# All 24 units make their first feed-forward layer in columns, with a new hand order of the work

## The chip, the cores and the metric

The kernel runs on one core of one Trainium2 chip. A core has five engines that run side by side, each working through its own instructions in order: PE (TensorE: matrix products), DVE (VectorE), ACT (ScalarE), POOL (GpSimd) and SP (SyncE, which here only issues transfers). 16 DMA engines move data between the chip's memory and the core. Products land in PSUM, eight banks that POOL cannot reach; all else lives in SBUF. The metric is the time of one execution on the device, in microseconds (us).

## What is computed

A linear attention with a decaying state (4 batches, 8 heads, 768 steps, head dimension 48), and behind it a feed-forward block with a softmax-weighted activation and a layer norm:

```
for t in range(S):                          # attention, for each batch and head
    y[t]  = r[t] @ (state + outer(u * k[t], v[t]))
    state = w[t][:, None] * state + outer(k[t], v[t])
x    = y of all heads side by side          # 3072 x 384
h    = x @ w_in                             # 3072 x 1024: the first layer
solu = h * softmax(h)
ln   = (solu - mean(solu)) / sqrt(var(solu) + 1e-6) * g_ln
out  = ln @ w_out                           # 3072 x 384
```

## The kernel before

The work is cut into 24 units of 128 tokens: unit i is chunk i // 4 of batch i % 4, and a unit needs the state that the unit four before it left. A unit goes through some forty steps. No loop orders them: the string `ORDER` is a list of words, written in the order in which the instructions are made, and `InOrder` (line 71) holds each engine to that order. So each engine does its words in the order of the string and waits where a word's data or buffer is not ready yet. A word is a step's name and the unit; behind the point stand the PSUM bank (for PE) or the engine that does it (a ACT, d DVE, p POOL; for loads, a means that ACT's queue issues it, else SP's). The words that matter here:

- `LW LK LR LV`: loads of w, k, r, v of a unit, 0.197 MB each, into rings of seven buffers. `LI0` to `LI2` load the three pieces of w_in (0.52 MB each), `LO` the halves of w_out (0.79 MB each); `wi` turns a piece of w_in into bf16, `gw` multiplies a piece of w_out by the gain, `mn`, `mc` and `ce` subtract its column mean.
- `lw` (logarithm of the decay, ACT), `cum` (its running sum, two products on PE), `ex` (exponential, ACT), `kp` (k and r scaled by it, DVE), `krk`, `krr` (both turned, PE) and `kr` (copied out of PSUM). For eight units `kt` turns them by a DMA of SP's queue instead.
- `M` (scores, 8 products), `m` (copied and masked; where ACT copies, POOL masks in a word `sel`), `vb` (v in bf16), `p q qh dg dv` (the bonus u, on POOL and DVE), `Y` (the attention's output, 12 products; a letter i means that the bonus is added by one product more on PE, n that `y` adds it on DVE), `y` (copied out), `S et st` (the state).
- `X` (y turned by PE into the bank) and `xT` (copied out); `xt` turns y by a DMA of SP instead, for units 21 to 23.
- `H`: the first layer. In columns it is 24 products, 8 blocks of 128 features by 3 pieces, and a unit's features lie on the partitions. `e` is its exponential (ACT), `he` h times e (DVE), `hq` the squares of he (ACT), `ea` the sum of the halves of e (POOL). `HA`/`HB` with `EA`, `DA`, `QA` and their like do the same for unit 23 in two halves.
- `Oa`, `Ob`: the two halves of the second layer. For a unit in columns each feature block gives a product on he (385 columns), one of width 1 on hq, and one on ea for every second block: the sums of e and of the squares come out of the same accumulation.
- `sq qm lv rs`: mean, variance and inverse root, on ACT and DVE; `o` scales the output, `out` stores it (SP).

Units 17 to 21 (set `by_rows`, those with a word `ht`) make the first layer in token rows: 6 products of 512 columns, tokens on the partitions. Then the sums of e and of the squares come out of ACT's own accumulation (`be_t`, `s2_t`; a word `sv` squares the sum of e), no `ea` is needed, and a DMA of SP's queue (`ht`, `turned_he`) turns he into columns for `Oa` and `Ob`, which then consist of the products on he alone.

PE's order in the last part before reads:

```
X18.4 Y20.n6 Y19.n0 M21.1 M22.3 H18.6 X20.0 Oa16.2 X19.1 Ob16 Y21.n1 H19.4 M23.6 Y22.n3 H20.0 Oa17.6
Y23.n7 Ob17 Oa18.3 H21.4 Ob18 H22.0 Oa19.2 HA23.6 Ob19 Oa20.7 HB23.3 Ob20 Oa22.4 Oa21.0 Ob22 Oa23.7 Ob21 Ob23
```

Of the kernel before, what the change touches and what calls it, by code (L numbers as in the profile page):

```python
# [8 lines left out]
F32 = mybir.dt.float32  # L9
# [12 lines left out]
ih0 LW0.a LU0.a LW2 LW5 LR2.a LW1.a LK1.a lw2 LW3 hot10.0 cum2.0 LR0.a LK2 LK0 p2 lw0 lw5 lw1 ik0 us0.3 cum0.4 ex2  # L22
LK3.a kp2 hot7.2 krk2.0 p0 LR3 krr2 LR1.a ex0 kp0 LV0.a kr2.d cum1.6 krk0.5 uc0 krr0 q0 p3 q2 ex1 lw3 hot2.0 cum3.3
LV2.a kr0.d LV3.a kp1 p1 M0.0 ex3 LK6 m0.a hot2.2 krk1.2 LW6 M2.6 LG0.a krr1 LR5 q1 qh1 LR6 dg0 LW7 kp3 krk3.1 dg2
krr3 LO1 vb0.p kr1.d LR7 cum5.4 vb2.p LK5.a LV1.a lw6 M1.2 m2.d vb3.p dv2 kr3.a hot3.0 cum6.6 ex6 dg1 m1.d hot1.0
M3.0 LW4.a S0.2 m3.d gs0.3 q3 S3.0 ex5 kp5 sel0 dv0 LK4.a p5 kp6 hot2.1 krk5.1 gc0 et3 lw7 Y2.n3 LK7 cum7.4 LO0
krk6.6 krr5 st3 y2.d et0 vb1.a st0 LR4.a gw5.a ex7 kr5.d dv1 LI1 Y0.i0 hot1.3 Y1.n2 LW9 y0.a lw4 q5 krr6 p6 LI2.a
hot2.1 cum4.0 ex4 kr6.d dg3 M5.6 q6 S1.3 LW8 kp7 gw6.a krk7.4 y1.d et1 X1.2 dv3 qh6 LI0.a Y3.i5 gw4.a kp4 p4 gw1.a
m5.d y3.a krr7 gw7.a hot1.0 X0.7 gw2.a kr7.d krk4.6 M6.0 X3.4 q4 krr4 xT0.d LV5.a gw0.d xT1.a LR9 gw3.d st1 xT3.a
LK11 mn0.5 kr4.d M4.3 p7 LR8 dg6 wi2.p LW11 S2.2 LV4.a wi0.d qh5 m6.a LK8 X2.1 LV6 mc0 xT2.a wi1.p ce4.d H3.6 dg4  # L30
m4.d ce5.p ce7.p LR11 vb5.a lw9 ce3.p e3 dg5 LK9 H0.0 H1.4 he3 vb4.a e0 ce2.p dv5 lw8 he0 e1 hq0.a Y5.n7 S4.6 y5.d
ce0.p et4 S5.3 ce6.p he1 H2.0 dv4 LV8 et5 Y4.n7 lw11 cum8.4 ce1.p st4 y4.d Oa0.6 ea1.p vb6.p p8 et2 hq1.a X5.7 st5
Ob0 st2 e2 ea2.p LW10 ex8 xT5.d LW12 he2 Oa1.7 cum11.2 sq0 qm0 kp8 cum9.0 Ob1 hq3.a lv0 rs0 ex11 ex9 sq1 o0.d lw10
S6.4 kp11 qm1 H5.5 q7 LR10 lv1 qh7 out0 et6 kp9 rs1 cum10.2 LK10 vb8.p o1.a M7.0 st6 ea3.p Oa3.7 e5 X4.4 dg7 ex10
LR12 m7.d Ob3 xT4.d hq2.a q8 dv6 sq3 p11 out1 lw12 H4.0 he5 qm3 qh8 lv3 rs3 Oa2.5 kp10 LK12 cum12.3 e4 o3.d krk11.6
dg8 sel6 krk8.2 krk9.7 hq5.a ex12 p10 LV7 krr8 q11 krr9 he4 kr8.d kp12 krr11 Ob2 kr9.a vb7.p M8.1 S8.0 LW14 S7.3
krk10.7 p9 sq2 qm2 lw14 ea4.p LV11 out3 q9 LR14 krk12.4 m8.d lv2 rs2 et8 krr10 o2.a st8 dv7 hq4.a kr10.d LW17 krr12
qh11 kr11.a Y6.n5 y6.d kr12.d cum14.0 Oa4.7 et7 st7 Y7.n2 ex14 y7.d lw17 LK14 ea5.p q10 out2 Ob4 vb11.a sq4 LW13
LV9 kp14 LR17 LK17 dv8 M9.5 m9.a M11.3 LV10 LK13 qm4 Y8.n2 S11.1 lv4 m11.d et11 Oa5.0 rs4 qh9 o4.a p12 lw13 cum17.4
ex17 dg10 y8.d p14 X7.7 krk14.3 X6.6 vb10.p out4 xT6.a dv10 Ob5 vb9.a krr14 dg11 st11 sq5 LR13 xT7.d kp17 kr14.a  # L40
M10.1 qm5 m10.d lv5 sel9 rs5 LW15 cum13.6 o5.d H6.4 ex13 M12.2 dg9 e6 H7.0 LV12 kp13 dv11 m12.a X8.6 Y11.n7 q12 e7
qh12 S9.2 he6 dv9 out5 LW16 LK15 y11.d S10.5 et9 xT8.a vb12.a lw15 M14.3 Y9.i6 Y10.n7 et10 lw16 he7 st9 st10
cum15.0 m14.d q14 sel12 ea7.p y9.a S12.2 hq7.a dg12 et12 H8.5 y10.d LR15 LV13 ex15 e8 p13 Oa7.3 dv12 X9.7 LR16 kp15
Ob7 he8 hq6.a krk15.4 LW18 ea8.p q13 sq7 qm7 st12 Y12.n0 xT9.a LW21 p15 y12.d krr15 LK16 lv7 LV14 lw18 cum16.5 p16
ea6.p rs7 o7.d X10.7 xT10.d H9.1 hq8.a kr15.d Oa8.7 X11.0 dg14 cum18.3 Ob8 ex16 e9 xT11.a lw21 kp16 he9 LR18 sq8
Oa6.5 X12.6 q15 vb14.p M15.1 ex18 out7 LV15 LK18 qm8 dg13 lv8 vb15.p vb13.p Ob6 m15.d rs8 o8.a sq6 qm6 S15.7
krk16.0 xT12.a lv6 LK21 kp18 rs6 et15 o6.a LR21 cum21.1 out8 S13.6 p18 q16 st15 et13 krr16 ex21 H11.3 hq9.a LW19
e11 LV17 ea9.p p17 st13 out6 kr16.d H12.5 kt13 LV16 kp21 lw19 dv14 ea11.p H10.0 dg15 LW20 he11 e12 he12 q17 q18
hq11.a dg16 dv15 LK19 Y14.n7 e10 LR19 ea12.p Oa9.2 y14.d hq12.a Oa11.3 M16.4 he10 M13.6 vb16.p Ob9 m16.a lw20 dv13
m13.d cum19.0 qh18 sq9 sel16 ex19 Ob11 sq11 LK20 LR20 qm9 kt17 lv9 qm11 rs9 lv11 kp19 ea10.p o9.a rs11 Y13.n7  # L50
vb17.p o11.a out9 S14.4 Y15.n6 et14 S16.5 et16 y15.d y13.d cum20.0 Oa12.2 out11 ex20 X15.3 st16 dg17 dv16 kp20 Ob12
X13.7 hq10.a p21 dv17 LW22 xT15.d sq12 p19 S17.5 qm12 xT13.a Y16.n0 M17.6 q19 st14 lv12 H13.3 rs12 o12.a y16.d
X16.2 LV18 lw22 m17.d et17 cum22.6 dg18 H15.0 e13 ex22 LK22 e15 vb18.p out12 LR22 xT16.d he13 kp22 he15 hq13.a
Oa10.2 H16.3 p20 LW23 lw23 q20 e16 X14.6 Ob10 st17 sq10 ea13.p ea15.p LK23 kt19 qh20 xT14.d qm10 hq15.a q21 LR23
he16 Y17.n0 Oa13.7 cum23.5 y17.d lv10 kt18 rs10 ex23 o10.d Ob13 sq13 qm13 lv13 rs13 X17.4 H14.0 o13.a kt20 e14
xT17.d kp23 M19.3 m19.d he14 M18.5 dv18 p23 m18.a Oa15.7 S18.2 Ob15 et18 dg21 p22 out10 sq15 M20.5 ea14.p qm15
hq14.a m20.d H17.0 dg20 out13 lv15 sel18 Y18.n4 LV20 LV19 st18 rs15 dg19 vb19.p kt21 vb20.p o15.a e17 Oa14.5 y18.d
dv20 dv19 S19.3 Ob14 X18.4 et19 he17 q22 hq16.a kt22 qh22 ea16.p Y20.n6 Y19.n0 st19 sq14 qm14 y20.d M21.1 xT18.a
q23 out15 M22.3 lv14 LV21 H18.6 y19.d m21.d kt23 vb21.p rs14 dg22 sv17 X20.0 Oa16.2 qh23 X19.1 Ob16 dv21 o14.a
out14 m22.d e18 he18 dg23 xT19.a LV22 xT20.a hq17.a sq16 sv18 Y21.n1 qm16 lv16 H19.4 vb22.p M23.6 y21.d dv22 Y22.n3  # L60
H20.0 rs16 m23.d LV23 y22.d ht17 o16.a e19 Oa17.6 hq18.a vb23.p ht18 xt21 dv23 Y23.n7 Ob17 e20 Oa18.3 he19 y23.d
out16 sq17 qm17 lv17 sv19 xt22 H21.4 hq19.a ht19 xt23 he20 rs17 Ob18 e21 ht20 H22.0 o17.d out17 sq18 qm18 Oa19.2
HA23.6 he21 lv18 rs18 e22 hq20.a Ob19 o18.d he22 EA23 sq19 Oa20.7 HB23.3 Ob20 sv20 qm19 hq22.a ht21 lv19 DA23 sq20
qm20 rs19 lv20 out18 o19.d ea22.p rs20 EB23 hq21.a Oa22.4 Oa21.0 o20.d QA23.d out19 DB23 Ob22 sq22 qm22 sv21 lv22
out20 Oa23.7 QB23.d Ob21 rs22 o22.a sq21 qm21 out22 lv21 rs21 Ob23 sq23 qm23 lv23 rs23 o21.d out21 o23.a out23
# [36 lines left out]
def kernel(  # L102
# [130 lines left out]
    diagonal = consts.tile([C, C], BF16)  # L233
# [335 lines left out]
    words = ORDER.split()  # L569
    squared = {int(word[2:].split(".")[0]) for word in words if word[:2] in ("hq", "QA")}  # L570

    def output(i, part):
        L = live[i]
        e, he, hq, o_ps = e_t[i % NWK], he_t[i % NWK], hq_t[i % NWK], L["o_ps"]
        for f in range(part * KF // 2, (part + 1) * KF // 2):
            if i in by_rows:
                pe.matmul(o_ps[:, :DM + 1], lhsT=he[:, f, :], rhs=w2[:, f, :], start=(f == 0), stop=(f == KF - 1))
                continue
            last = f == KF - 1 and i not in squared
            pe.matmul(o_ps[:, :DM + 1], lhsT=he[:, f, :], rhs=w2[:, f, :], start=(f == 0), stop=last and i in added,  # L580
                      skip_group_check=True)
            if i not in added:
                pe.matmul(o_ps[:, DM + 1:DM + 2], lhsT=e[:, f, :], rhs=inv_col, start=False, stop=last,
                          skip_group_check=True)
            elif f % 2 == 0:
                pe.matmul(o_ps[:, DM + 1:DM + 2], lhsT=ea_t[i % NWK][:, f // 2, :], rhs=inv_col, start=False, stop=False,
                          skip_group_check=True)
            if i in squared:
                pe.matmul(o_ps[:, DM + 2:], lhsT=hq[:, f, :], rhs=one_col[:, :1], start=False, stop=(f == KF - 1),
                          skip_group_check=True)  # L590
            else:
                pe.matmul(L["g_ps"], lhsT=he[:, f, :], rhs=he[:, f, :], start=(f == 0), stop=(f == KF - 1))

    def output_a(i, x):
        if i in squared:
            live[i]["o_ps"] = bank([C, DM + 3], F32, x, "o_ps")
        else:
            both = bank([C, 2, 512], F32, x, "o_ps")
            live[i]["o_ps"], live[i]["g_ps"] = both[:, 0, :DM + 2], both[:, 1, :C]
        output(i, 0)  # L600
# [11 lines left out]
    def variance(i, x):  # L612
        if i not in squared:
            dve.scalar_tensor_tensor(out=diagonal, in0=live[i]["g_ps"], scalar=sq_t[i % NWK][:, 0:1], in1=ident,
                                     op0=SUB, op1=MULT, accum_out=qm_t[i % NWK])
            return
# [34 lines left out]
    for word in words:  # L651
# [33 lines left out]
```

## Time and profile before

| | us |
|---|---|
| median of 3 runs (153.36 to 154.04) | 153.54 |
| the profiled execution | 153.27 |
| its span, from the first instruction to the last | 151.5 |
| busy: PE, DVE, ACT, POOL | 133.4, 122.1, 119.9, 115.2 |
| DMA: read, written | 22.03 MB, 4.72 MB |
| first product of a first layer (H3) starts | 38.24 |
| last output (Ob23) ends on PE | 147.2 |

The profile numbers times from the start of the span. A row of an engine's instructions in order of time has the start, the duration, the engine, the line, what is written and read, and in brackets the idle time of the engine ahead of it with what ended that. All instructions carry the line of `InOrder`'s call (L87), so they are told apart by what they write and read: `ps<-xT,win_sb` is H in columns, `ps<-win_sb,xT` H in rows, `ps<-w,he` the wide product of the second layer, `ps<-one_col,hq` that on the squares, `e<-ps` the exponential, `hq<-win_f` or `hq<-he` the squares of a unit in rows or in columns. Products overlap, so what one costs is the time from its start to the start of the next.

### The profile page before, as it was taken

To read this page: it belongs to the slowest core of one execution; us is meant where nothing else is said; L and a number is where in the kernel's file an instruction comes from. 1 tells how busy PE (TensorE), PEld (TensorE's weight loads), DVE (VectorE), ACT (ScalarE), POOL (GpSimd) and SP (SyncE) were. 2 spreads that over 40 slices of the span, in tenths; PEclk is the share of its full clock that TensorE was granted. 3 is DMA by queue.
4 is the path that set the end of the run, shared out by engine and by line. 5 is a ranking of instruction groups with operands and counts; after the bars stand their busy time and mean duration, and the time that the engine had idled before them with its cause. 6 is when DMAs were issued, how large, how long until landed. Compare 5 with 4: busy or idle time off the path is not lost.

```text
span 151.5 us, 4749 instructions
## 1 busy us (share of the span) xinstructions
PE 133.4 (88%) x1853; PEld 95.2 (63%) x1858; DVE 122.1 (81%) x215; ACT 119.9 (79%) x258; POOL 115.2 (76%) x154
## 2 busy tenths in 40 slices
PE   6977877549999999996999999979999999996980
PEld 2333444425996788775888689658867675565650
DVE  5047998397899999997999999879688998868550
ACT  3355656734899999996999989988988877997782
POOL 7159997686999999995999999999986599603000
PEclk9999999955999999999999999999999999999997
DMA  5999999999993489998989999999988997957533
GB/s 100 258 259 259 259 326 299 376 315 220 197 208 58 100 183 240 209 205 197 222 165 211 212 225 135 229 200 219 234 164 210 174 204 159 202 149 151 123 146 114
DMA packets 119800, 30.75 MB, mean 203 GB/s; under 512 B 115289, under 2 KB 119394, under 8 KB 119778
## 3 DMA queue, kind: packets, MB, share of 16 engines
q1 hardware_dynamic: 101792, 26.06, 80.8%
q10 hardware_dynamic: 17986, 4.40, 12.6%
q8 instruction: 14, 0.23, 0.6%
q14 instruction: 8, 0.07, 0.1%
HBM read 22.03 MB, written 4.72 MB: 176 GB/s over the span
## 4 chain that ended last, share of the span: by engine, by line
PE 25%; POOL 21%; DMA 20%; ACT 13%; ACTq 6%; issue 5%; DVE 4%; SPq 3%; DVEq 0%; POOLq 0%
PE ps L87 25%; DMA kr_in<-in_r_dram 7%; ACTq L87 6%; POOL ea L87 5%; DMA v_in<-in_v_dram 5%; POOL q L87 4%; SPq L87 3%; POOL w L87 3%; DMA kr_in<-in_k_dram 3%; ACT e L87 3%; POOL dv L87 3%; DMA xT<-y 3%; POOL p L87 2%; DMA w_in<-in_w_dram 2%; DVE kp L87 2%
## 5 line engine op out<-in xcount | busy, mean ns | idle before, releaser
L87 PE MATMUL ps<-w,he 128*128 128x385 bf16 x192 | 42.9, 325 | 0.0
L87 DVE TENSOR_TENSOR kp<-ps,kr_in 128x768 bf16<-128x768 f32 x24 | 22.8, 953 | 14.2 <-ACT ps L87 5.7
L87 PE MATMUL ps<-xT,win_sb 128*128 128x128 bf16 x456 | 28.1, 219 | 2.4 <-DVE kp L87 1.3
L87 POOL TENSOR_TENSOR p<-kr_in 128x384 bf16<-128x384 f32 x24 | 24.0, 1004 | 7.3 <-DMA kr_in<-in_k_dram 4.2
L87 PEld LDWEIGHTS <-win_sb 128*128 128x128 bf16 x456 | 26.1, 98 | 3.9 <-DMA xT<-y 1.5
L87 ACT ACTIVATE e<-ps 128x1024 bf16<-128x1024 f32 (+1 forms) x25 | 24.6, 985 | 2.5 <-PE ps L87 0.9
L87 POOL TENSOR_TENSOR ea<-e 128x512 bf16<-128x512 bf16 x17 | 19.6, 1157 | 7.4 <-ACT e L87 7.4
L87 PE MATMUL ps<-one_col,hq 128*128 128x1 bf16 x152 | 24.9, 164 | 0.0
L87 DVE TENSOR_TENSOR he<-ps,e 128x1024 bf16<-128x1024 f32 (+1 forms) x20 | 23.3, 1165 | 1.2 <-ACT e L87 0.9
L87 DVE TENSOR_TENSOR m<-ps,keep 128x1024 bf16<-128x1024 f32 x18 | 21.8, 1216 | 0.8 <-PE ps L87 0.8
L87 POOL TENSOR_TENSOR q<-p,u_bc 128x384 bf16<-128x384 bf16 x24 | 21.9, 915 | 0.6 <-DMA kr_in<-in_k_dram 0.2
L87 ACT ACTIVATE ps<-ps 128x768 f32<-128x768 f32 x24 | 19.0, 800 | 4.0 <-PE ps L87 2.4
L87 PEld LDWEIGHTS <-he 128*128 128x128 bf16 x192 | 18.2, 96 | 5.8 <-DVE st L87 0.2
L87 POOL TENSOR_TENSOR dv<-vb,dg 128x384 bf16<-128x384 bf16 x24 | 19.9, 832 | 1.3 <-ACT vb L87 1.0
L87 ACT ACTIVATE hq<-he 128x1024 bf16<-128x1024 bf16 x18 | 18.9, 1051 | 0.0
L87 ACT ACTIVATE lw<-w_in 128x384 bf16<-128x384 f32 x24 | 12.3, 522 | 6.8 <-issue 5.3
L87 PEld LDWEIGHTS <-kp 128*128 128x128 bf16 x208 | 13.0, 99 | 7.3 <-DVE kp L87 5.8
L87 PEld LDWEIGHTS <-hq 128*128 128x128 bf16 x152 | 11.6, 96 | 5.5
L87 PE MATMUL ps<-ident,kp 128*128 128x128 bf16 x128 | 11.0, 225 | 3.4 <-DVE kp L87 3.4
L87 PEld LDWEIGHTS <-kr 64*128 64x128 bf16 (+1 forms) x272 | 10.2, 96 | 5.4 <-issue 1.9
L87 POOL CAST vb<-v_in 128x384 bf16<-128x384 f32 x18 | 8.9, 506 | 4.5 <-DMA v_in<-in_v_dram 4.0
L87 PE MATMUL ps<-warm 128*128 128x512 bf16 x28 | 9.8, 468 | 2.0 <-DVE kp L87 1.7
(94 smaller groups left out, 286.3 us busy)
## 6 DMA issues: line engine op xcount, KB each, us to landing
out_dram<-o SPq DMA_DIRECT2D x24, 192.0 KB, 2.9
w_in<-in_w_dram SPq DMA_DIRECT2D x21, 192.0 KB, 4.4
kr_in<-in_k_dram SPq DMA_DIRECT2D x20, 192.0 KB, 4.1
kr_in<-in_r_dram SPq DMA_DIRECT2D x20, 192.0 KB, 4.4
v_in<-in_v_dram SPq DMA_DIRECT2D x18, 192.0 KB, 4.2
wout_f<-in_moe_w_out_dram SPq DMA_DIRECT2D x2, 768.0 KB, 7.1
v_in<-in_v_dram ACTq DMA_DIRECT2D x6, 192.0 KB, 5.5
win_f<-in_moe_w_in_dram ACTq DMA_DIRECT2D x2, 512.0 KB, 6.4
```

What stands on the lines that cost most here:

```text
L87: made = make(*args, **kwargs)
```

## The change

No word `ht`, `sv` is left, so `by_rows` is empty: units 17 to 21 go in columns like all others, and each gets a word `ea`. Unit 0, which summed e by eight products of its own, gets an `ea` too (`ea` is then there for all but unit 23). Unit 20's y is turned by DMA (`xt20` for `X20`, `xT20`). The whole string `ORDER` is another permutation: 941 words instead of 950. In it

- DVE, ACT and POOL exchange words: of the 24 `vb`, ACT has 12 (6 before) and POOL 12; `kr` 2 on ACT and 14 on DVE (4 and 12); `gw` 7 on ACT and 1 on POOL (6 on ACT, 2 on DVE); `ce` 4 and 4 on DVE and POOL (1 and 7); `wi` on ACT, POOL, POOL (POOL, POOL, DVE); `xT` 14 on ACT and 6 on DVE (12 and 9); `qh` 10 (12). The six `sel` are for other units.
- `Y1` and `Y10` add the bonus on PE and `Y9` no longer does.
- The weights' loads stand elsewhere among the others: `LO1 LV2 LO0` and `LI0 LI1 LW8 LI2` follow each other, where before it was `LO1`, five loads, `LO0`, and `LI1 LW9 LI2 LW8 LI0`. `LR5` goes to ACT's queue, `LW4` to SP's.
- `hot`, products that nobody reads, which keep PE busy at the start: 33 instead of 31.

In the code only dead paths go: the product of he with itself, which would give the squares of units without `hq` (none), and its buffer `diagonal`.

```diff
-    words = ORDER.split()
-    squared = {int(word[2:].split(".")[0]) for word in words if word[:2] in ("hq", "QA")}
...
-            last = f == KF - 1 and i not in squared
-            pe.matmul(o_ps[:, :DM + 1], lhsT=he[:, f, :], rhs=w2[:, f, :], start=(f == 0), stop=last and i in added,
+            pe.matmul(o_ps[:, :DM + 1], lhsT=he[:, f, :], rhs=w2[:, f, :], start=(f == 0), stop=False,
                       skip_group_check=True)
...
-            if i in squared:
-                pe.matmul(o_ps[:, DM + 2:], lhsT=hq[:, f, :], rhs=one_col[:, :1], start=False, stop=(f == KF - 1),
-                          skip_group_check=True)
-            else:
-                pe.matmul(L["g_ps"], lhsT=he[:, f, :], rhs=he[:, f, :], start=(f == 0), stop=(f == KF - 1))
+            pe.matmul(o_ps[:, DM + 2:], lhsT=hq[:, f, :], rhs=one_col[:, :1], start=False, stop=(f == KF - 1),
+                      skip_group_check=True)
```

The new order, from PE's Ob16 on and by engine, as the words stand in the string:

```
PE   Ob16 X19.1 cum23.6 Y18.n4 H19.1 Oa17.0 Oa14.3 M21.6 M20.4 Ob17 X18.1 Ob14 Y21.n7 H18.1 Oa19.4 M22.6 Ob19 S19.5
     Y20.n0 M23.1 H21.6 Y22.n3 Oa18.4 Y23.n5 Ob18 H20.2 Oa21.0 H22.6 Ob21 HA23.1 Oa20.2 HB23.3 Ob20 Oa22.5 Oa23.7 Ob22 Ob23
ACT  sq16 lv16 rs16 ex23 hq17.a e19 hq14.a vb21.a sq17 xT18.a sq14 hq19.a lv17 rs17 lv14 e18 rs14 m22.a sq19 o14.a et19
     lv19 rs19 vb22.a vb23.a e21 hq18.a sq18 lv18 rs18 e20 hq21.a e22 sq21 hq20.a lv21 rs21 EA23 hq22.a sq20 EB23 lv20
     rs20 o20.a sq22 lv22 sq23 rs22 lv23 rs23 o23.a
SP   kt21 out15 LR23 kt20 out16 LV21 LV20 kt22 kt23 xt21 LV22 LV23 out17 out14 xt20 out19 xt22 xt23 out18 out21 out20 out22 out23
```

And PE and ACT from unit 4's loads on to the first layers (a star marks a transfer that ACT issues):

```
PE   krk6.4 krr6 S2.4 krk5.6 X0.7 Y2.n2 krk4.3 krr5 M6.0 krr4 Y1.i4 mn0.7 S3.2 Y3.i6 X2.4 krk7.0 krr7 hot2.1 M5.4 X3.6 X1.3 H0.0 H3.6
ACT  gw4.a LR4.a* gw7.a gw5.a LV3.a* gw3.a ex5 LI0.a* gw6.a ex7 et2 gw1.a gw0.a LI2.a* et1 xT0.a vb3.a kr5.a LV4.a* y1.a mc0
     LV5.a* y3.a et3 xT2.a wi2.a lw8 xT3.a xT1.a lw11 e0
```

## The prediction

> **What bounds the kernel now.** I read the page first: busy times, then the span in slices.
>
> ```profile
> span 151.5 us, 4749 instructions
> ...
> PE 133.4 (88%) x1853; PEld 95.2 (63%) x1858; DVE 122.1 (81%) x215; ACT 119.9 (79%) x258; POOL 115.2 (76%) x154
> ...
> PE   6977877549999999996999999979999999996980
> ...
> PEclk9999999955999999999999999999999999999997
> DMA  5999999999993489998989999999988997957533
> GB/s 100 258 259 259 259 326 299 376 315 220 197 208 58 100 183 240 209 205 197 222 165 211 212 225 135 229 200 219 234 164 210 174 204 159 202 149 151 123 146 114
> ```
>
> One slice is 3.8 us. For the first ten PE has holes while the DMA engines are full: the start waits for loads. From slice 11 (38 us) to slice 39 PE is at 9 nearly throughout: there the kernel lasts as long as PE's own work plus its few waits. Slices 9 and 10 ran at half clock. From there on any wait of PE is paid in full, so next I read PE in order of time, and looked for idle time.
>
> ```profile
> 70.20 1.50 PE L87 MATMUL ps<-xT,win_sb 128*128 128x128 bf16 x24 [1.29 <-DVE kp L87]
> ...
> 100.67 0.34 PE L87 MATMUL ps<-lw,uti_neg 128*128 128x384 bf16 x1 [0.78 <-DVE kp L87]
> ...
> 113.92 0.34 PE L87 MATMUL ps<-ident,y 128*128 128x128 bf16 x3 [0.52 <-DVE y L87]
> ...
> 126.02 0.18 PE L87 MATMUL ps<-inv_col,ea 128*128 128x1 bf16 x1 [0.29 <-POOL ea L87]
> ...
> 133.78 1.46 PE L87 MATMUL ps<-win_sb,xT 128*128 128x512 bf16 x6
> 135.07 0.82 PE L87 MATMUL ps<-w,he 128*128 128x385 bf16 x4
> 135.73 1.50 PE L87 MATMUL ps<-xT,win_sb 128*128 128x128 bf16 x24
> 137.07 0.82 PE L87 MATMUL ps<-w,he 128*128 128x385 bf16 x4
> 139.05 0.84 PE L87 MATMUL ps<-xT,win_sb 128*128 128x128 bf16 x12 [1.16 <-DMA xT<-y]
> ```
>
> Brackets hold idle time and what ended it. After 40 us the waits over 0.15 us are these five, 4.04 us together. The rows from 133.78 on price PE by the start of the next row: a first layer in token rows 1.29 us (H21), one in columns 1.34 (H22). A half output of a row unit costs 0.66 (135.07 to 135.73); one of a column unit 0.81, from eight halves seen in the same view. The other words, in the same way: M 0.33, Y 0.37, cum 0.32, HA 0.67, X 0.165.
>
> Last, ACT at the end, for what stands between a first layer and an output.
>
> ```profile
> 130.28 1.02 ACT L87 ACTIVATE e<-ps 128x1024 bf16<-128x1024 f32 x1
> 131.18 0.20 ACT L87 ACTIVATION_READ_ACCUMULATOR e<-ps 128x1 f32 x1
> 131.28 1.05 ACT L87 ACTIVATE hq<-win_f 128x1024 bf16<-128x1024 bf16 x1
> ...
> 137.27 1.02 ACT L87 ACTIVATE e<-ps 128x1024 bf16<-128x1024 f32 x1
> ```
>
> e19 takes 1.02 us and hq18 starts as it ends. H22 starts at 135.73 and its e22 at 137.27, with ACT free: 1.54 us from the start of H to the start of e.
>
> **The change, term by term.** The profiled execution took 153.27 us (span 151.5, 1.8 around it); the median of the runs is 153.54. The sum is made against 153.27.
>
> *PE work, +1.5.* Units 17 to 21 go to columns: 0.05 for the first layer and 2 x 0.15 for the output, 5 x 0.35 = +1.75. Unit 0 now adds on POOL: four short matmuls fewer, -0.1. X20 goes, -0.165. One unit more adds its bonus on PE (Y1 and Y10 for Y9), +0.17. Sum 1.65; bounds 1.4 (if the wide and the narrow first layer cost the same) and 1.75; I take 1.5. All lies where PE is dense. The two warm-up matmuls more lie in the start, where PE waits.
>
> *Waits at the end, +4.3.* A row unit's output reads only he, which the DMA turns; its squares go into ACT's sum and reach no matmul. A column unit's output has as third matmul, 0.19 us after its first, one on hq, the squares that ACT makes. So units 17 to 21 now have ACT between the first layer and PE, and the order puts the squares late: on ACT "e19 hq14", "e21 hq18", "e20 hq21" and "e22 sq21 hq20" stand directly behind each other. ACT takes its words in order, so hq waits for an e of another unit, and that e for its H. From the start of H, hq ends at 1.54 + 1.02 + 1.05 = 3.61. PE reaches the third matmul after what stands between:
> - Oa14: H19 1.34, Oa17 0.81, 0.19 = 2.34: waits 1.27.
> - Oa18: H21 1.34, Y22 0.37, 0.19 = 1.90: waits 1.71.
> - Oa21: directly behind H20, 1.53: waits 2.08.
> - Oa20: H22 1.34, Ob21 0.81, HA23 0.67, 0.19 = 3.01, with 0.12 more for sq21: waits 0.72.
>
> Each counts from its own H, so they add: 5.78. They are floors, for ACT may be late at an e as well. Between Ob14 and e21 it has sq14, hq19, lv17, rs17, lv14, e18, rs14, m22, sq19, o14, et19, lv19, rs19 and two vb, 6.7 us by its rows, while PE's words up to the end of H21 take 6.2; with 0.1 to sq14 and 0.2 from H to e that makes e21 0.4 late. As much at each of the four gives 7.4. Before, the end had 0.29 (Oa16) and 1.16 (HA23), and both go: ea16 has more work before it, and xt23 no longer stands behind ht19 on SP. 5.78 - 1.45 = +4.3; bounds 3.9 (0.1 us of reading error at each) and 5.9.
>
> Unit 20's turn by DMA I cost at nothing: page part 6 has 3.9 us from issue to landing for xT<-y, with y20 0.75 after Y20: 4.7. PE has M23, H21, Y22, Oa18 with its wait, Y23 and Ob18 in between: 5.7. Without Oa18's wait the cover is 4.0, and 0.7 us would show. xt23 has 7.2 of PE time as cover for 5.9 (y23, the issue of xt22, its own 3.9). Six more ea at 1.157 us cost nothing either: POOL stands idle 6.33 us before ea22, and 12 instead of 18 vb are left to it. If ACT, which gets these six vb (0.51 each), delays a kr or m by one, 0.5 us.
>
> *Start, -1.4.* Before, DVE's kp4 starts at 30.67, 0.12 us after LR4 landed (30.55), and from it PE runs on through X0, M6, X3, the column mean, M4 and X2 to the first H at 38.24. LR4 is now behind 6.69 MB of loads instead of 7.08, and the last piece of w_in behind 8.85 instead of 9.05. At 258 GB/s that is 1.5 us and 0.8 us. PE work ahead of the first H, its words at their prices, is 13.3 us instead of 13.4. I take LR4's 1.5 less 0.1. Lower end -4.1: only w_in holds H, landing at 32.8 with a 1.1 us cast behind (33.9 against 38.24, less what xT3 and xT1 behind it hold up). Upper end +1.5: ACT now makes wi2 (1.1), gw0, gw3 and kr5 (1.0) ahead of H0, against m6 (1.0) and gw2 before, and the issues of the last w_in loads stand behind gw in its queue.
>
> *Middle, -1.3.* The 0.78 before cum20 ended with kp19, which waited for LR19. That load is now behind 20.8 MB of transfers instead of 21.0, and kp19 behind 71.6 us of PE work instead of 70.2. The 0.52 before X17 goes, as PE has 5.4 us of work between Y17 and X17 instead of 1.9. H6's 1.29 stays: kp17's last load is 0.6 MB later, its use 2.8 us. Bounds -2.6 (that one goes too) and +2.6: outside these waits PE loses 2.6 us in shorter ones (from Oa0 at 45.6 to X17 at 113.9 there are 63.1 us of work and 2.6 of the waits shown), and the new order, with DVE, ACT and POOL all above 90% from 40 us on, could double them.
>
> Sum: 153.27 + 1.5 + 4.3 - 1.4 - 1.3 = 156.4. The tail behind the last output (sq, qm, lv, rs, o, out23) is the same.
>
> **Rivals.** *Tight start, no change:* LR4 and ACT are not what holds H0, only w_in, and PE keeps its clock; the gain at the start is 4.1 and pays for the waits: 156.4 - 2.7 = 153.7. For: part 2 has the DMA engines full up to the first H, and 1.7 us of idle PE at 31.68. Against: ACT's longer list there.
>
> *Faster:* in addition the middle runs without waits. The whole of H6's 1.29 goes, and half of the short ones: 153.7 - 1.3 - 1.3 = 151.1. Decides from the point where the start gains over 3.5 us and loads keep ahead from 50 us on. Against: the loads follow buffers that come free with the compute.
>
> *Half clock at the end:* the trace shows 6.83 us at half clock from 30.37 on, after a stretch (26.8 to 30.2) in which PE was busy 1.96 of 3.4 us. From the wait of Oa18 to that of Oa21 there are 1.71 and 2.08 us of idling around 3 us of work. If that halves the clock for as long, 3.4 us come on top: 159.8. Against: after 1.29 and 1.16 us of idling (70 and 139 us) it stayed full.
>
> The Trainium skill (TensorE: Matmul & The Clock Gate, What's actually happening) has the clock halve after a whole idle window of about 3.4 us. By that rule the end keeps its clock, and 156.4 stands; the halving at 30.37 does not agree, since no hole of PE before it lasted over 1.8 us.
>
> That the order is not what the words say is excluded: in the built program ACT's row for the exponential of unit 20 stands directly ahead of the square of unit 21.
>
> **Numbers.** Forecast 0.59, tight start 0.14, faster 0.13, half clock 0.14. A difference under 0.5% (152.8 to 154.3 around the median) can't be told from none here. Faster: the third case and a little of the second, 0.14. Within: most of the second, some of the first, 0.13. Slower 0.73. The terms' distances to their bounds, as the root of their squares, are 3.0 down and 5.2 up; half of that gives the forecast's own range, 154.9 to 159.0. For 8 in 10 it reaches down to 152.8, over the tight start, and up to 159.4; left out are the faster case and half of the half clock.
>
> **What would show it.** PE rows with an idle time on hq ahead of an output at Oa14, Oa18, Oa21 and Oa20 of about 1.3, 1.7, 2.1 and 0.7, ended by ACT hq; no wait on a DMA of xT ahead of the last first layers; the first H at about 36.8; PE's work up by 1.5. I am wrong if the first H comes before 34.5, or if those waits are not there. If PE's clock falls below full after 120 us, the third rival holds.

## The result, and the profile after

The changed kernel takes 161.87 us (median of 4 runs, 158.62 to 163.88) against 153.46 for the kernel before (4 runs beside it, 153.36 to 154.04): a ratio of 1.0443, 95% interval 1.0344 to 1.0541. It is slower, and by more than forecast; 161.87 lies above the range. Its runs also lie 5 us apart, those of the kernel before 0.7. Runs over 1.5% above the fastest of their kernel count as slow and ratios leave them out, so a ratio can differ from the quotient of the medians; the execution shown below, of 162.77 us, is a slow one.

The page of the changed kernel: span, busy times, and three rows of the span in 40 slices of 4.0 us.

```profile
span 161.0 us, 5029 instructions
...
PE 137.3 (85%) x2001; PEld 104.0 (65%) x2004; DVE 123.5 (77%) x214; ACT 121.8 (76%) x251; POOL 116.6 (72%) x150
...
PE   6956781798999999999896999999997995759970
...
PEclk9999999659999999999999999999999999695997
DMA  5999999999983899999797989998899936120112
```

To slice 30 (121 us) the picture is the old one, with one dip of PE in slice 22 (85 us). Then PE falls to 5, 7 and 5 in slices 34 to 36, and the granted clock to 6 and 5 in slices 35 and 37, where before it was at 9 from slice 11 to the last but one. The DMA engines are at 2 or less from slice 35 on, so it is not their throughput that holds the end.

PE of the changed kernel in order of time, the rows with idle time ahead of them (those over 0.3 us from 28 us on, except 0.52 at 79.86 and 0.77 at 29.59):

```profile
28.26 0.40 PE L87 MATMUL ps<-ident,kp 128*128 128x128 bf16 x4 [2.65 <-DVE kp L87]
...
38.54 0.66 PE L87 MATMUL ps<-xT,win_sb 128*128 128x128 bf16 x9 [0.51 <-DVE kr L87]
...
86.23 0.32 PE L87 MATMUL ps<-lw,uti_neg 128*128 128x384 bf16 x1 [1.35 <-ACT lw L87]
...
124.92 0.18 PE L87 MATMUL ps<-one_col,hq 128*128 128x1 bf16 x1 [0.90 <-ACT hq L87]
...
135.20 0.36 PE L87 MATMUL ps<-vb,m 128*128 128x48 bf16 x8 [0.56 <-ACT vb L87]
137.78 0.18 PE L87 MATMUL ps<-one_col,hq 128*128 128x1 bf16 x1 [2.04 <-ACT hq L87]
144.67 0.18 PE L87 MATMUL ps<-one_col,hq 128*128 128x1 bf16 x1 [1.89 <-ACT hq L87]
150.39 0.18 PE L87 MATMUL ps<-one_col,hq 128*128 128x1 bf16 x1 [0.37 <-ACT hq L87]
```

From the third row on, 1.35, these replace the five waits of before (1.29, 0.78, 0.52, 0.29, 1.16). The rows on `one_col,hq` are those that were forecast: PE stands in an output before the product on the squares, at Oa14 (0.90), Oa18 (2.04), Oa21 (1.89) and Oa20 (0.37). Two more were not forecast: 0.30 at Oa17 just ahead of Oa14, and the 0.56 on `vb`, which is Y22.

ACT of the changed kernel around those waits:

```profile
134.64 0.51 ACT L87 CAST vb<-v_in 128x384 bf16<-128x384 f32 x1 [1.34 <-DMA v_in<-in_v_dram]
...
135.76 1.02 ACT L87 ACTIVATE e<-ps 128x1024 bf16<-128x1024 f32 x1
136.67 1.05 ACT L87 ACTIVATE hq<-he 128x1024 bf16<-128x1024 bf16 x1
...
142.65 1.02 ACT L87 ACTIVATE e<-ps 128x1024 bf16<-128x1024 f32 x1 [0.89 <-PE ps L87]
143.57 1.05 ACT L87 ACTIVATE hq<-he 128x1024 bf16<-128x1024 bf16 x1
```

The squares of unit 18 (136.67) start as the exponential of unit 21 ends, and those of unit 21 (143.57) as that of unit 20 ends. The `he` that they read had long been there: he18 was made at 130.99 to 132.22. What PE waits for at 137.78 is an operation whose input was ready some four microseconds before it started. The first row shows ACT itself idle for 1.34 us on the load of unit 22's v; H21 starts at 132.95, so e21 comes 2.81 behind it instead of 1.54.

The same end by stretches of 3.413 us: time, then busy time (number of instructions) of PE, PEld, DVE, ACT, POOL, then the granted clock, the share of the DMA engines and GB/s.

```profile
134.82:138.23 3.41, 0.98 (x17) 0.62 (x17) 2.44 (x3) 2.71 (x4) 2.77 (x3) 1.00 0.54 160
138.23:141.64 3.41, 3.41 (x37) 2.55 (x36) 0.72 (x2) 0.55 (x3) 0.00 (x0) 0.50 0.14 32
141.65:145.06 3.41, 1.52 (x23) 1.16 (x21) 1.84 (x2) 2.08 (x3) 1.15 (x1) 1.00 0.16 59
145.06:148.47 3.41, 3.41 (x33) 3.06 (x32) 0.00 (x0) 0.17 (x1) 0.00 (x0) 0.50 0.02 5
```

Each of the two long waits leaves PE busy for 0.98 and 1.52 us of a stretch, and the next stretch runs at half clock. PE is then busy all 3.41 us, but its work takes longer: H22, at 145.49, needs 2.51 us to the start of the next word instead of 1.34. By the prices of the words in them, the two stretches lose about 1.55 us each, 3.1 together (an estimate from the starts of the rows).

Where the 9.50 us between the two profiled executions (153.27 and 162.77) lie, by the start of a PE word less the work of all PE words ahead of it at the prediction's prices (before: 24.83 at the first H, 30.09 at H17, 31.81 at the last output; after: 25.28, 29.01, 39.22):

| | forecast | measured |
|---|---|---|
| PE's own work | +1.5 | +1.4 |
| lost time to the first H | -1.4 | +0.45 |
| from there to H17 (middle) | -1.3 | -1.5 |
| from H17 to the last output, without half clock | +4.3 | +5.4 |
| half clock there | 0 | +3.1 |
| behind the last output | 0 | +0.7 |
| sum | +3.1 | +9.5 |

Of the 5.4, 4.05 are the waits on squares (5.50) less the two old waits at the end (1.45), and 0.56 is Y22. Of the 0.7 behind the last output the place is known and the cause is not: SP is done with out23 1.9 us after PE's end in both traces, and the span ends 3.1 us after that instead of 2.4. All eleven traces with the new order have this 3.1, the three with the old one have 2.4 to 2.6.

### The profile page after: what moved, and what is told of

It is laid out like the page before. It is cut to its first block, busy times and chain, and to the rows that moved or that the text cites. A ratio compares the mean times of both kernels' runs of the same rounds, so it can differ in the third digit from the quotient of the medians.

```text
span 161.0 us, 5029 instructions
## 1 busy us (share of the span) xinstructions
PE 137.3 (85%) x2001; PEld 104.0 (65%) x2004; DVE 123.5 (77%) x214; ACT 121.8 (76%) x251; POOL 116.6 (72%) x150
## 3 DMA queue, kind: packets, MB, share of 16 engines
q10 hardware_dynamic: 17986, 4.40, 11.9%
## 4 chain that ended last, share of the span: by engine, by line
PE 36%; DMA 25%; ACT 18%; DVE 7%; SPq 6%; issue 4%; POOL 2%; DVEq 0%; ACTq 0%
PE ps L87 36%; DMA w_in<-in_w_dram 9%; SPq L87 6%; DMA wout_f<-in_moe_w_out_dram 5%; DMA v_in<-in_v_dram 5%; ACT e L87 4%; ACT hq L87 3%; DMA kr_in<-in_k_dram 3%; DMA kr_in<-in_r_dram 3%; ACT lw L87 2%; ACT o L87 2%; ACT vb L87 1%; DVE kp L87 1%; ACT lv L87 1%; POOL dv L87 1%
## 5 line engine op out<-in xcount | busy, mean ns | idle before, releaser
L87 PE MATMUL ps<-w,he 128*128 128x385 bf16 x192 | 46.6, 331 | 0.0
L87 PE MATMUL ps<-xT,win_sb 128*128 128x128 bf16 x576 | 37.4, 225 | 0.5 <-DVE kr L87 0.5
L87 POOL TENSOR_TENSOR ea<-e 128x512 bf16<-128x512 bf16 x23 | 26.5, 1155 | 15.3 <-ACT e L87 10.8
L87 PE MATMUL ps<-one_col,hq 128*128 128x1 bf16 x192 | 31.8, 166 | 5.6 <-ACT hq L87 5.5
L87 PEld LDWEIGHTS <-win_sb 128*128 128x128 bf16 x576 | 34.6, 101 | 2.0 <-issue 1.0
L87 DVE TENSOR_TENSOR he<-ps,e 128x1024 bf16<-128x1024 f32 (+1 forms) x25 | 29.0, 1176 | 2.8 <-ACT e L87 2.6
L87 DVE TENSOR_TENSOR kp<-ps,kr_in 128x768 bf16<-128x768 f32 x24 | 22.5, 952 | 10.7 <-ACT ps L87 7.3
L87 POOL TENSOR_TENSOR p<-kr_in 128x384 bf16<-128x384 f32 x24 | 24.0, 1001 | 8.5 <-DMA kr_in<-in_r_dram 6.4
L87 ACT ACTIVATE e<-ps 128x1024 bf16<-128x1024 f32 (+1 forms) x25 | 24.6, 985 | 6.0 <-PE ps L87 5.3
L87 ACT ACTIVATE hq<-he 128x1024 bf16<-128x1024 bf16 x23 | 24.2, 1050 | 0.1
L87 PEld LDWEIGHTS <-hq 128*128 128x128 bf16 x192 | 14.5, 97 | 13.5 <-ACT hq L87 6.6
L87 DVE TENSOR_TENSOR m<-ps,keep 128x1024 bf16<-128x1024 f32 x18 | 21.8, 1217 | 1.3 <-PE ps L87 1.3
L87 POOL TENSOR_TENSOR dv<-vb,dg 128x384 bf16<-128x384 bf16 x24 | 19.9, 831 | 3.6 <-ACT vb L87 3.3
L87 POOL TENSOR_TENSOR q<-p,u_bc 128x384 bf16<-128x384 bf16 x24 | 21.7, 913 | 0.4
L87 PEld LDWEIGHTS <-he 128*128 128x128 bf16 x192 | 18.6, 97 | 4.5 <-issue 0.2
L87 ACT ACTIVATE ps<-ps 128x768 f32<-128x768 f32 x24 | 19.1, 800 | 1.0 <-PE ps L87 0.9
L87 PEld LDWEIGHTS <-kp 128*128 128x128 bf16 x208 | 13.6, 99 | 7.5 <-DVE kp L87 4.2
L87 ACT ACTIVATE lw<-w_in 128x384 bf16<-128x384 f32 x24 | 12.3, 522 | 4.4 <-DMA w_in<-in_w_dram 4.4
L87 PE MATMUL ps<-inv_col,ea 128*128 128x1 bf16 x92 | 15.4, 167 | 0.0
L87 PE MATMUL ps<-ident,kp 128*128 128x128 bf16 x128 | 11.4, 227 | 4.4 <-DVE kp L87 3.2
L87 PEld LDWEIGHTS <-kr 64*128 64x128 bf16 (+1 forms) x272 | 10.3, 96 | 5.0 <-issue 2.6
L87 DVE TENSOR_TENSOR y<-ps,dv 128x384 bf16<-128x384 f32 x20 | 10.9, 551 | 2.3 <-PE ps L87 1.4
```

The lines of the kernel that those rows point to most:

```text
L87: made = make(*args, **kwargs)
```

## The experiments

Times are medians, beside runs of the kernel before on the same chip; a ratio is to these. Where the order string takes more lines, the call's line is L91 instead of L87.

### The squares ahead of the exponentials

```diff
-out16 e19 hq14.a
+out16 hq14.a e19
-st19 vb22.a ... e21 dv23 Y22.n3 hq18.a
+st19 hq18.a vb22.a ... e21 dv23 Y22.n3
-Ob18 sq18 ... e20 hq21.a
+Ob18 hq21.a sq18 ... e20
-Oa21.0 H22.6 e22 ... he22 hq20.a
+Oa21.0 hq20.a H22.6 e22 ... he22
```

> The changed kernel (161.9 us, 158.6 to 163.9) with four words moved on ACT: hq14 ahead of e19, hq18 ahead of vb22, hq21 ahead of sq18, hq20 ahead of H22's e22. Theory A (the second layer waits for squares that stand behind another unit's exponential, and the idling halves PE's clock): PE has no wait over 0.5 us ahead of Oa14, Oa18, Oa21 and Oa20, the clock stays full from 40 us to the last output, and the time is 153.5 to 155.5. Rival B (at the end PE waits for loads and for y turned by DMA, and the squares only come last): 158 or more, the same idle time ended by other things. Rival C (the new order loses its time at the start and in the middle): over 159.

154.62 us (153.48 to 155.55), ratio 1.0161 (1.0072 to 1.0251). PE's waits that are left from 127 us on, and the clock's row of its page:

```profile
131.97 0.36 PE L91 MATMUL ps<-vb,m 128*128 128x48 bf16 x8 [0.55 <-ACT vb L91]
...
139.69 0.83 PE L91 MATMUL ps<-xT,win_sb 128*128 128x128 bf16 x12 [0.84 <-DMA xT<-y]
...
143.39 0.18 PE L91 MATMUL ps<-one_col,hq 128*128 128x1 bf16 x1 [0.42 <-ACT sq L91]
...
PEclk9996999869999999999999999999999999999996
```

Four words moved on one engine take away 6 to 7 us by the medians (161.87, and 160.92 in the last experiment), 4.3 us by the ratios (1.0443 to 1.0161). The waits on the four late squares are gone (0.30 at Oa17 stays), the clock stays full from 32.8 us to the last products, and the waits that come up behind are others: Y22's `vb`, the turn of y23 by DMA (0.84), which the longer waits had covered, and 0.42 ahead of unit 22's squares, which ACT ends at 143.34.

### The waits filled with unread products

```diff
-xt20 Oa18.4
+xt20 hot9.0 Oa18.4
-he20 Oa21.0
+he20 hot9.1 Oa21.0
```

> The changed kernel with nine products that nobody reads (128 x 512, 0.22 us each) ahead of Oa18 and nine ahead of Oa21, on banks 0 and 1, which are free there; every wait stays. Theory A: PE is busy in its waits, its clock stays full after 40 us, the waits for the squares are filled, and what the half clock cost at the end (about 3 us of the profiled run) goes: 157.5 to 159.5, with a spread of under 1.5 us between runs. If idling is not what halves the clock: 160 to 164 and slices below 9 in PEclk after 130 us.

157.9 us (156.08 to 159.01), ratio 1.0341 (1.023 to 1.0452). Two stretches of 3.41 us at the end (columns as above):

```profile
133.82:137.23 3.41, 2.74 (x24) 1.39 (x23) 2.66 (x3) 2.89 (x4) 2.76 (x3) 1.00 0.52 163
...
140.65:144.06 3.41, 3.41 (x38) 2.23 (x36) 1.23 (x1) 1.61 (x2) 1.15 (x1) 1.00 0.20 60
```

PE does nothing useful sooner, the outputs wait for the squares as before, yet by the medians 3 to 4 us go: with PE kept busy the clock is 1.00 from 34.8 us to the last products. By the ratios it is only 1.6 us (1.0443 to 1.0341), and their intervals overlap, so the times alone do not settle the size; that the two spells of half clock are gone stands in the trace. So part of what the late squares cost is the clock that falls because of the waits: between a quarter and two fifths, with 1.6 of 6.6 us by the ratios or 3 to 4 of 9 to 10 us by the medians (next experiment).

### The outputs without the squares

```diff
-pe.matmul(o_ps[:, DM + 2:], lhsT=hq[:, f, :], rhs=one_col[:, :1], ...
+pe.matmul(o_ps[:, DM + 2:], lhsT=(he if i in (14, 18, 20, 21) else hq)[:, f, :], rhs=one_col[:, :1], ...
```

For these four units the narrow product reads `he`, which PE's wide products have waited for anyway.

> The changed kernel in which the narrow product of units 14, 18, 20 and 21 reads he in the place of hq: the sums of squares of these units are left out (they become sums of he), PE does the same number of products of the same sizes, and ACT still makes every hq. Theory A: the same as with the squares moved, 153.5 to 155.5, as nothing but that wait is taken away. Rival B: 158 or more. If it is faster than the kernel with the squares moved by over 1 us, moving them costs something elsewhere.

152.18 us (151.41 to 153.88, 10 runs), ratio 1.0013 (0.9963 to 1.0063).

```profile
PE   6997794498999999999999999899999989989960
...
PEclk9999999559999999999999999999999999999998
```

PE is at 8 and 9 to the last outputs, and the clock at 9 from slice 10 on. All the same work is done on every engine; only what four outputs wait for is changed, and the loss is gone. Whatever else the new order does, it costs nothing that can be measured beside this. The time is 2.4 us below that with the squares moved (ratios 1.0013 and 1.0161), so moving them costs something in its turn. About 1.0 us of it can be placed: y23's turn is waited for 0.25 us here instead of 0.84, and nothing is ahead of unit 22's squares instead of 0.42.

### Columns in the old order

The kernel before without its words `ht17` to `ht21` and `sv17` to `sv21`, and with `ea17` to `ea21` behind the exponential of the same unit.

> The kernel before (153.5 us) with units 17 to 21 in columns and nothing else moved: the words ht and sv go, each of the five units gets an ea on POOL behind its e. Theory A (the order, not the columns as such, makes the waits): PE work up by 1.75, the wait of 1.16 ahead of HA23 gone, one new wait of about 1.8 ahead of Oa21 (hq21 stands behind EB23): 155 to 156.5. Rival D (columns at the end cost by themselves, because every output then needs ACT's squares, whatever the order): 158 or more, with waits ahead of Oa18 and Oa19 too.

157.87 us (156.35 to 158.2), ratio 1.0359 (1.0274 to 1.0445). The two longest of PE's waits from 100 us on:

```profile
111.08 0.33 PE L91 MATMUL ps<-ident,y 128*128 128x128 bf16 x3 [1.60 <-DVE kp L91]
...
147.75 0.18 PE L91 MATMUL ps<-one_col,hq 128*128 128x1 bf16 x1 [1.46 <-ACT hq L91]
```

Oa21 waits for its squares (1.46), Oa18 and Oa19 do not, so the sign of rival D is absent. Of the rest, 1.60 stands at X14, ahead of all units that were changed, and 0.81 at Oa16. That is about 2 us more than the middle of what I had expected, and mixed in cause: X14 also waits in another run of the old order (0.88 in the one with the start filled); why it waits longer here is not shown. What the run shows is only that columns without their own order are no gain.

### The holes of the start filled

```diff
-ex7 S2.4 dv2 kp5 kp4 krk5.6
+ex7 hot3.5 S2.4 dv2 kp5 kp4 hot11.5 krk5.6
-gw2.p Y2.n2
+gw2.p hot3.5 Y2.n2
```

The unread products land on a bank that holds unit 1's new state until it is copied, so that state is changed; the work is the same.

> The changed kernel with unread products put into PE's three holes at the start: three ahead of S2, eleven ahead of krk5 (it idled 2.65 us there) and three ahead of Y2. Nothing else is moved. Theory A (the start lost its forecast gain to half clock: kp4 came 2.1 us earlier than before, but PE's words from 29.0 to 35.8 us ran at half speed): the clock stays full from 5 us to the end's holes, those words cost about 2.4 us less, the first H starts at about 36.3 (35.5 to 37.0) instead of 38.54, and the whole takes about 159.8. Theory B (the last cast of w_in and the copies ahead of it hold the first H, whatever PE's clock): the first H stays at 38.0 or later and the time at 161 to 162.

159.48 us (156.66 to 160.08; 152.72 before). The clock's row and the first H:

```profile
PEclk9995699999999999999999999999999999569996
...
36.50 1.67 PE L91 MATMUL ps<-xT,win_sb 128*128 128x128 bf16 x27 [0.82 <-DVE kr L91]
```

The half clock from 29 to 36 us is gone (there is an earlier spell, from 11.9 to 18.8) and the first H starts at 36.50 instead of 38.54, although `kp4` starts no earlier (28.66; 28.58 in the changed kernel). Theory A: the copies and casts ahead of H0 were late because PE was slow (the last cast of w_in starts at 34.66, in the changed kernel at 37.01). What ends PE's wait before H0 is in both traces DVE's copy `kr7`. Ahead of it DVE stands idle for the column mean, whose products PE made at half clock in the changed kernel (2.43 us) and at full clock here (0.57).

### Squares first and start filled together

The edits of the first and the fifth experiment; the same state is changed.

> The four squares moved ahead of the other units' exponentials, as in the experiment with the squares first (154.6 us), and the start's holes filled as well. If both losses are what they seem and add: first H at about 36, no half clock before the end, 152.6 us (151.8 to 153.4), about level with the kernel before. If the start is held by loads and casts: 154.0 to 154.8. If the later clock state makes the end halve instead: over 155.

152.78 us (152.08 to 155.07, 10 runs), ratio 1.0043 (0.9995 to 1.0091), with the first H at 36.58. The two effects add (1.0161 with the squares alone), and give back what the change lost, no more.

### The start of the kernel before filled

```diff
-hot2.1 cum4.0
+hot5.1 cum4.0
-gw6.a krk7.4
+gw6.a hot4.1 krk7.4
-hot1.0 X0.7
+hot7.1 hot3.0 X0.7
```

The four products ahead of krk7 overwrite half of unit 4's decays.

> The kernel before with its start's holes filled by unread products: five instead of two ahead of cum4, four ahead of krk7, and seven and three instead of one ahead of X0. Theory A (half clock from 30.4 to 37.2 us costs the kernel before as well): the clock stays full, the first H (H3) starts at 36.0 to 36.8 instead of 38.24, and the whole takes about 151.5 (0.98 to 0.995 of before). Theory B (w_in, landed at 32.8 and cast by 33.9, and the loads behind it hold what follows): the first H gains less than 0.5 us, or what it gains is lost again at the waits for loads in the middle, and the time stays within 0.5%.

152.16 us (151.07 to 155.01, 10 runs), ratio 0.9971 (0.9926 to 1.0015): no difference that can be told. The clock stayed full from 25.8 us, and from X0 to the first H the words took 3.7 us instead of 5.4. But my ten products ran from 31.63 to 33.78, so X0 started 1.0 us later than before, and H3 came at 37.50, 0.74 earlier, between the two theories; the middle then waited a little more (X14 0.88). Too much filling ate more than half of what the clock gave.

### One wait filled

```diff
-xt20 Oa18.4
+xt20 hot9.0 Oa18.4
```

> The changed kernel with nine unread products ahead of Oa18 only; the hole of Oa21 stays. Theory A (each hole halves the clock by itself, for 3.4 us): the half clock that began at 138.2 is gone, the one that began at 145.1 behind Oa21's hole stays, and the time lies between the changed kernel (161.9) and the one with both holes filled (157.9), at about 160. Theory B (the two holes halve it together, as the idle time adds up over some 10 us): no half clock between 100 us and the last products, 157.5 to 158.5. Theory C (the half clock follows no hole): both spells stay, 161 to 163.

159.76 us (157.28 to 160.66; 152.72 before). The stretch with Oa21's wait and the next:

```profile
138.08:141.49 3.41, 1.51 (x26) 1.29 (x24) 1.87 (x3) 2.55 (x5) 1.05 (x1) 1.00 0.31 91
141.50:144.91 3.41, 3.41 (x32) 2.94 (x31) 0.12 (x1) 0.00 (x0) 0.09 (x1) 0.50 0.00 0
```

One spell is left, behind the hole that is left: each hole halves the clock by itself. That rests on the trace; the times lie between those of both holes and of none, but overlap with either.

### Half of each wait filled

The second experiment with four unread products in each place instead of nine (`hot4.0`, `hot4.1`).

> The changed kernel with four unread products (0.9 us) instead of nine ahead of each of Oa18 and Oa21, so that holes of about 1.0 us are left of 2.0 and 1.9. Theory A (the granted clock halves where PE is busy for less than about half of a window of 3.41 us: in the traces all 23 windows below 0.46 halved, and of some 90 above 0.55 one did): windows there are busy 0.6 or more, the clock stays full from 36 us to the last products, and the time is that of the filled holes, 157.9 (156 to 159). Theory B (a hole of about 1 us is enough, as at the start): half clock at the end stays at least once, 160 to 162.

157.22 us (156.32 to 157.43), ratio 1.0327 (1.0238 to 1.0415). The two stretches with what is left of the holes, 1.14 us ahead of Oa18's product and 1.03 ahead of Oa21's:

```profile
133.51:136.91 3.40, 2.26 (x34) 1.44 (x32) 2.16 (x4) 1.70 (x2) 1.98 (x3) 1.00 0.32 91
136.92:140.32 3.40, 2.69 (x35) 1.92 (x33) 1.60 (x4) 2.38 (x5) 0.61 (x1) 1.00 0.30 90
```

PE is busy for 66% and 79% of them and the clock stays full. Four products do as much as nine.

### The loads of v earlier

```diff
-LV20 ... kt22 ... kt23 ... xt21 ... LV22 ... LV23
+LV20 ... LV22 LV23 kt22 ... kt23 ... xt21
```

> The changed kernel with the loads LV22 and LV23 ahead of kt22 on SP instead of behind xt21; nothing else. Theory A (ACT's exponential of unit 21 was 1.1 us late as vb22 and vb23, behind late loads, stand ahead of it, so Oa18 waited for that too): the 0.56 us ahead of Y22 go, e21 starts 1.5 us after H21 instead of 2.8, hq18 ends about 1.2 us earlier, Oa18 waits about 1.7 us behind Y22 and the time falls by about 1.2 us, to 160.5 (158 to 162 by its spread). Theory B (e21 waits for the first layer only): Y22's wait goes and Oa18's grows by as much, the end is where it was.

156.62 us (156.35 to 158.99, 5 runs), ratio 1.029 (1.0155 to 1.0424). ACT in the execution of 158.56 us:

```profile
131.72 0.91 ACT L91 CAST vb<-v_in 128x384 bf16<-128x384 f32 x2
133.07 1.02 ACT L91 ACTIVATE e<-ps 128x1024 bf16<-128x1024 f32 x1 [0.44 <-PE ps L91]
133.99 1.05 ACT L91 ACTIVATE hq<-he 128x1024 bf16<-128x1024 bf16 x1
```

The casts no longer wait, and the exponential now waits for PE: e21 starts 1.61 behind H21 (131.46), not 2.81, and Oa18 stands 1.58 us. That is theory A, worth 1.2 us beside the execution of 162.77 us and 0.6 beside that of 158.91 us in the last experiment, where e21 comes 2.22 behind H21. By the medians the time fell by 4.3 to 5.3 us instead (against 160.92 and 161.87), by the ratios by 2.3 (1.0443 to 1.0290). In this execution only one stretch of the end ran at half clock, which is about 1.6 us more: the wait of Oa18 (133.51 to 135.09) lies across a boundary of the stretches, at 134.57. With that the ratios are accounted for, the medians are not.

### All three cures

The first experiment's order; unread products of 112 columns that lie in a free strip of a bank at the start (12, 45 and 12, so nothing is overwritten); `LV22 LV23` ahead of `kt22`, and `xt22 xt23` ahead of `out19`.

> The four squares moved ahead of the other units' exponentials, the start's holes filled by unread products of 112 columns that lie in a free strip of a bank (12, 45 and 12 of them), and on SP the loads LV22 and LV23 ahead of kt22 and the turns xt22 and xt23 ahead of the store out19. If what is left of waits at the end (about 4.1 us from unit 17's first layer on, of them 0.6 on the late vb22 and 0.6 and more on y turned by DMA) stems from that queue: about 151.2 us (150.4 to 152.0), 0.98 to 0.995 of the kernel before. If those waits are replaced by others (the squares are still one behind the other on ACT): 152.4 to 153.2, no difference to before.

152.64 us (152.04 to 153.81, 12 runs) against 153.33 (150.74 to 155.05), ratio 1.0036 (0.9997 to 1.0075): the second of the two expectations. H0 came at 35.92, the clock was full from 10.7 us to the end. But:

```profile
128.37 0.40 PE L91 MATMUL ps<-kr 64*128 64x128 bf16 x8 [0.84 <-DMA kr<-kp]
...
143.49 0.18 PE L91 MATMUL ps<-one_col,hq 128*128 128x1 bf16 x1 [0.75 <-ACT sq L91]
```

The 0.84 is M22, whose turn `kt22` is now two loads later on SP. The wait went from Y22 to M22, and the one ahead of unit 22's squares grew from 0.42 to 0.75. No version beat the kernel before by more than the noise.

### The changed kernel again

> The changed kernel itself once more, beside the kernel before, since the four runs shown of it lie between 158.6 and 163.9 us and the single edits were timed on other occasions. Theory A (its spread is that of the windows of 3.41 us: the same holes of 1.9 and 2.0 us halve the clock in one, two or more windows, by how they lie to the windows, and a late load in the middle comes and goes): again a spread of several us, with a lower granted clock in the longer runs, median 159 to 162.5; in the trace every half window follows one in which PE was busy for less than half. Theory B (the time is fixed, and the spread was that chip's): all runs within 1 us.

160.92 us (158.43 to 161.99, 6 runs), 153.22 before. The end of the execution of 158.91 us by stretches:

```profile
132.00:135.42 3.42, 1.42 (x26) 1.05 (x25) 2.22 (x4) 2.01 (x3) 2.31 (x3) 1.00 0.35 99
135.42:138.83 3.41, 3.41 (x33) 3.02 (x31) 1.25 (x3) 0.67 (x3) 0.00 (x0) 0.50 0.13 29
138.83:142.25 3.42, 1.53 (x23) 1.10 (x21) 1.23 (x1) 1.97 (x2) 1.15 (x1) 1.00 0.18 62
142.25:145.66 3.41, 3.41 (x33) 2.72 (x30) 0.11 (x2) 1.33 (x3) 0.58 (x1) 0.50 0.00 0
```

The same two holes (2.00 and 1.89), the same two spells. So the shorter of the two traced executions has them too; the 3.9 us between this execution and the one of 162.77 lie elsewhere: 1.0 at the start (one stretch at half clock instead of two, first H at 37.50), 2.1 in the middle (no 1.35 ahead of cum18), the rest at the end. The spread of several us is there again, as theory A has it, and every half stretch follows one in which PE was busy for less than half. One part of theory A failed: the longer runs do not have the lower granted clock (158.43 us at 0.948, 160.89 at 0.963).

## Why the prediction was right and wrong, step by step

*Direction and main mechanism: right.* The waits on `hq` stand at the four outputs named, for the reason named. Forecast 1.27, 1.71, 2.08 and 0.72, together 5.78; measured 0.30 and 0.90 (Oa17, Oa14), 2.04, 1.89 and 0.37, together 5.50. The experiments with the squares first and without the squares take away 6 to 7 and 9 to 10 us by the medians, 4.3 and 6.6 by the ratios. One reading in the sum was off by 0.1: behind a unit in columns the squares start 0.91 us after the exponential (135.76 to 136.67), not 1.02.

*What failed, first: the half clock was left a rival.* The forecast took the waits at their own length. So the step that failed is the one that priced a wait at its length alone: the clock behind the waits cost about 3.1 us more. The rival had the right place and, by luck, nearly the right price (3.4 us; it supposed one spell of 6.8 us, and there were two of 3.41), but got a chance of 0.14. Two arguments held it down. One was that the clock stayed full after idle times of 1.29 and 1.16 us. I compared holes where I should have compared busy shares: the stretches of 3.41 us around those two had PE busy for 2.12 and 2.25 us in the trace of before (62% and 66%), the two at the end of the changed kernel 0.98 and 1.52 (29% and 45%). In the trace of before (columns as above):

```profile
67.92:71.33 3.41, 2.12 (x35) 1.62 (x33) 2.14 (x4) 2.38 (x6) 1.54 (x4) 1.00 0.84 189
136.18:139.59 3.41, 2.25 (x33) 1.73 (x31) 3.05 (x4) 2.83 (x8) 1.15 (x1) 1.00 0.69 117
```

From prices alone this was to be had: 3.41 less a wait of 1.7 to 2.1 is 38 to 50%, and the row I quoted for the halving at 30.37 had 1.96 of 3.4, 57%.

The other was the rule of the Trainium skill (TensorE: Matmul & The Clock Gate, What's actually happening), by which the clock halves after a whole idle window. The trace does not agree: PE was idle for no more than 2.04 us at a stretch ahead of either spell. The measurement decides here, and the row at 30.37 had already said so.

*What failed, second: the start, -1.4.* The load's part was right: `kp4` came 2.1 us earlier (28.58 against 30.67), more than the 1.5 taken. The step that PE's work ahead of the first H is 13.3 us instead of 13.4 is true too, but it is the work behind the late load that counts. At the prediction's prices it is about 4.6 us now (krk4 to X1) and was 3.2 (X0 to X2), and the half clock, up to 35.84, fell on it. With the clock kept full the first H comes at 36.50, where 36.8 was forecast. So the missing 1.85 us are again the clock, which fell behind the waiting ahead of krk5: 2.65 us in one place in this execution, 0.70 and 1.43 in the second one. The gain stayed away in all eight traces of the changed kernel whose start was left as it is: their first H lies between 37.50 and 38.74.

*The end beyond this.* The late e21 was foreseen in kind (0.4 us, for ACT's own load) and not in cause: SP issues LV22 at 130.43, behind `xt21`, and 12 `vb` on ACT put the exponentials behind that load. I had costed these `vb` at half a microsecond, in case they delay a kr or m; what they delayed was an e. Unit 20's turn by DMA cost nothing, as said, and neither did the `ea`: PE waits for neither.

*Middle, -1.3 against -1.5:* right in the sum, partly by chance. The 0.78, the 0.52 and nearly all of H6's 1.29 went, and 1.35 ahead of cum18 and 0.52 at 79.86 came. In the second execution of the changed kernel these did not come, and the middle lost 1.6 us instead of 3.7.

*The rivals.* The half clock held (159.8; with the start's failure, 1.85, and the late load it is the result). "No change" and "faster" fell, since nothing paid for the waits.

## What to carry to other kernels

Read an in-order engine's list for operations that are ready but stand behind one that is not: four squares behind another unit's exponential cost 4 to 7 us here, and moving four words cured it. On TensorE, price a wait by what it leaves of the stretch around it: two waits of 2 us cost 2 us each and about 1.55 us more each through the clock, while four unread products in the hole, which gain nothing by themselves, kept the clock full. And a load that comes earlier is worth only what the work behind it leaves, at the clock at which that work runs.

## What the runs showed of the hardware

The granted clock changed only at multiples of 3.413 us from its first change, in all 14 traces. I cut each trace into these stretches and compared PE's busy share of one with the clock of the next:

```
clock full, PE busy     stretches   halved in the next
under 46%                   37            37
46% to 66%                  21             3
over 66%                   506             0
clock half, PE busy     stretches   full in the next
up to 85%                   11             0
from 88%                    26            26
```

So here a stretch in which PE idles for over 54% halves the clock every time, in however many pieces the idling comes (in one such stretch, busy for 36%, no piece was longer than 0.90 us), and a nearly full one brings it back. Between 46% and 66% the busy share does not decide alone: 3 of 21 halved, one of them at 65%. A hole of 2 us that lies within a stretch cost about 1.55 us more. One that straddles a boundary can cost nothing more: 1.58 us across the boundary at 134.57, with the loads of v earlier, left the clock full. But 2.10 us across that at 134.81, with the start filled, halved it, since 1.50 of them and 0.37 ahead of Y22 fell into one stretch. The Trainium skill (TensorE: Matmul & The Clock Gate, What's actually happening) gives the window as 3413 ns and as free-running, and with both the traces agree; with its condition, an idle window, they do not: in 35 of the 40 stretches that halved the clock PE was at work for a part.

The same holes can therefore cost more or less from run to run, by how they lie to the stretches. How much of the changed kernel's spread this is stays open: its ten runs lie between 158.4 and 163.9 us and their granted clocks between 0.938 and 0.963, but the clock does not order the times, and of the 3.9 us between the two traced executions 2.1 lie in the middle, at full clock. The kernel with all three cures, at full clock from 10.7 us on in its trace, stayed within 1.8 us in twelve runs.
